# Block one's bands read q and k from the pooled branch's pieces; band matmuls in 64x64 and 128x64 tiles

## The chip, the cores and the metric

One core of a Trainium2 chip runs the whole program in one launch. The metric is the device time of one execution in microseconds, the median of three runs. The kernel before takes 1001.09 us (1000.05 to 1003.14).

## What is computed

Attention over 4 batches, 8 heads, 576 positions and 64 dimensions, followed by two expert layers (512 to 2048 to 512) on the 2304 tokens. The attention has two branches that are added. The pooled one averages q, k and v over groups of four positions and attends over 144; its result is repeated four times. The local one lets each position see only those less than four away:

```
q_d, k_d, v_d = mean over 4 positions of q, k, v
out_up    = repeat(softmax(q_d k_d' / 8) v_d, 4)
scores    = where(|i - j| < 4, q k' / 8, -1e9)
out_local = softmax(scores) v
x  = out_up + out_local                 # 2304 x 512
x  = relu(x @ w_in)^2 @ w_out           # layer 1
h  = x @ w2_in;  out = (h * cos(h)) @ w2_out   # layer 2
```

## The kernel before, in words

**Tiles.** Two heads lie on the 128 partitions (head pair hp of four, 64 dimensions each). The local branch goes by bands (`window(w)`): 64 query positions and the 70 keys around them (67 at a batch's edge), 9 bands a batch, 36 in all. A band loads one tile with q and k of all four pairs (`qkw`, L367) and one with v (`vw`, L372). In `qkw`, q of a pair stands as a 128x128 block with zeros off the diagonal, so that one 128x128 matmul scores both heads of a pair at once: rows 0 to 63 of the score bank are head one's positions, rows 64 to 127 head two's. L379 first writes the mask into the bank (identity times the band mask, bfloat16), L383 adds the scores, one float32 matmul for each pair. The softmax follows (`exps`, L273 to L290), the division on POOL (L393), the transposes of each pair (L403), the copy to SBUF (L406, `pt`), and L420 multiplies v with it, again 128x128 for each pair: of the output, the two diagonal 64x64 blocks are used. L436 adds the pooled result and writes x, L448 and L449 split x into a high and a low part.

**The pooled branch.** `pool(b)` loads q and k of a batch in eight pieces (128x576, one for each of q, k and pair, L200) and v in further pieces (L203), and VectorE sums groups of four (L260, L265, L267). `down(b, hp)` scores a pair (L303), transposes (L324), copies (L331, `dpt`), multiplies with v (L336) and copies the result out (L345, `xd`). A band's product with v waits until all four pairs of its batch are done.

**The layers.** `conv1(f)` loads a raw weight tile (1 MB, L461) and decodes it into a high and a low tile (L475 to L496). The main loop does, for each block of tokens and each of 16 weight tiles, 12 matmuls of `stage_a` (L568) and 12 of `stage_b1` (L620) or as many rows of `stage_b2` (L626). Block one of layer 1 is the first eight bands; the other 28 are computed beside the main loop's matmuls of earlier blocks, and are started at slots of that loop.

**Order.** Ahead of the main loop (`early[0]` is true) the program runs in rounds over a list of generators: `pool(0)`, four `down(0, hp)`, `window(0)` to `window(7)`, three `conv1`. Each goes on until it lacks a buffer or ends a stage. `need` and `done` count buffers (`caps`); in this phase the names in `SPREAD` may also take one of 13 spare tiles, those of weight tiles 3 to 15, which nobody has filled yet. Pooled pieces take only spare tiles, and give them back as soon as their sum is issued. Between the rounds a few matmuls on constants (`warm`, L697) are issued on TensorE. From this order the framework makes each engine's own program, by simulated times; at run time each engine keeps to its program and waits on semaphores. All DMAs are issued by SyncE (SP), in order.

Of the kernel before, what the change touches and what calls it, by code (L numbers as in the profile page):

```python
# [8 lines left out]
F32 = mybir.dt.float32  # L9
# [9 lines left out]
P = 128  # L19
B, H, S, D = 4, 8, 576, 64  # L20
FACTOR = 4
SD = S // FACTOR
HALO = FACTOR - 1
HPAIR = H // 2
WQ = 64
WK = WQ + 2 * HALO
# [27 lines left out]
TOP_MIN = 2.0 ** -15  # L54
TOP_MAX = (2.0 - 2.0 ** -3 - 2.0 ** -23) * 2.0 ** 16
LO_RING = (("loa", AHEAD), ("lob", AHEAD + LAG))
SPREAD = ("pl", "qkw", "vw", "dpr", "dpt")
RANK = {"down": 0, "window": 1, "pool": 2, "conv1": 3, "conv2": 3}


# [8 lines left out]
def kernel(  # L69
# [43 lines left out]

    caps = {
        "a": 3, "h": 1, "acc": 4, "qkw": 3, "vw": 3, "pr": 3, "pt": 2, "xt": 1, "qp": 1, "xd": 2, "vp": 1, "av": 3, "pl": 2, "raw": 2,
        "dpr": 2, "dpt": 1,
    }
    used = dict.fromkeys(caps, 0)
    now = [-1]
# [3 lines left out]

    def need(name, n=1):
        while early[0] and name in SPREAD:
            if name != "pl" and used[name] < caps[name]:
                used[name] += 1
                held.setdefault(name, []).append(None)
                return
            if spare:  # L130
                held.setdefault(name, []).append(spare.pop(0))
                return
            yield
        while used[name] + n > caps[name]:
            yield
        used[name] += n

    def done(name, n=1):
        f = taken[name].pop(0) if early[0] and name in SPREAD else None
        if f is None:  # L140
            used[name] -= n
        else:
            spare.append(f)
# [33 lines left out]


    pooled = {}
    xds = {}  # L180
    qk_used = {}
    vp_used = {}
# [5 lines left out]
    def pool(b):  # L188
        yield from need("qp")
        yield from need("vp")  # L190
        kp = cm.tile([P, HPAIR, SD], F32, tag="kp", name="kp", bufs=caps["qp"])
        vp = cm.tile([KTOK, 2, DM], F32, tag="vp", name="vp", bufs=caps["vp"])
        parts = [(i, hp) for hp in range(HPAIR) for i in range(2)]
        parts += [((0, 1), hp) for hp in range(HPAIR)] if early[0] else [((kt,), hp) for hp in range(HPAIR) for kt in range(2)]
        loaded = []
        for i, hp in parts:
            yield from need("pl")
            if isinstance(i, int):
                t = task_tile("pl", P, S)
                nc.sync.dma_start(out=t, in_=pool_qk[b, i, hp])  # L200
            else:
                t = task_tile("pl", KTOK, len(i) * FACTOR * P)
                nc.sync.dma_start(  # L203
                    out=t.rearrange("p (k c) -> p k c", k=len(i)),
                    in_=pool_v[b, hp, :, i[0]:i[-1] + 1],
                )
            loaded.append((i, hp, t))
            if len(loaded) < 2:
                continue
            if not early[0]:  # L210
                yield
            if b < PE_POOLED:
                if not early[0]:
                    yield
                bank, = yield from need_a()
                pe_pool(bank, loaded, kp, vp)
                done_a(bank)
                done("pl")
                done("pl")
                loaded = []  # L220
            while loaded:
                pool_sum(*loaded.pop(0), kp, vp)
                done("pl")
        pooled[b] = (qp, kp, vp)

    def pe_pool(bank, pieces, kp, vp):
# [25 lines left out]
    def pool_sum(*piece):  # L252
        with behind("gl", "xl"):
            pool_piece(*piece)
# [107 lines left out]
    def window(w):  # L362
        b, i, t0, k0, k1 = window_of(w)
        n, off = k1 - k0, HALO - (t0 - k0)
        yield from need("qkw")
        qk = task_tile("qkw", P, HPAIR * (2 * WQ + WK))
        nc.sync.dma_start(out=qk, in_=win_qk[w])  # L367
        qw = qk[:, :HPAIR * 2 * WQ].rearrange("p (h m) -> p h m", h=HPAIR)
        kw = qk[:, HPAIR * 2 * WQ:].rearrange("p (h s) -> p h s", h=HPAIR)
        yield from need("vw")  # L370
        vw = task_tile("vw", WK, DM)
        nc.sync.dma_start(out=vw, in_=win_v[w])  # L372
        yield
        if not early[0]:
            yield
        yield from need("pr")
        s, = yield from need_a()
        sv = s[:, :HPAIR * n].rearrange("p (h s) -> p h s", h=HPAIR)
        nc.tensor.matmul(  # L379
            sv, ident_b, band[:, off:off + n].unsqueeze(1).broadcast_to([P, HPAIR, n]), start=True, stop=False  # L380
        )
        for hp in range(HPAIR):
            last["pe"] = nc.tensor.matmul(  # L383
                sv[:, hp], qw[:, hp], kw[:, hp, :n], start=False, stop=hp == HPAIR - 1
            ).ins
        done("qkw")
        mx = cm.tile([P, 2, HPAIR], F32, tag="mx", name="mx", bufs=4)
        pr = cm.tile([P, HPAIR, WK], F32, tag="pr", name="pr", bufs=caps["pr"])
        prv = pr[:, :, :n]
        yield from exps(s, sv, mx, prv, SCALE)  # L390
        nc.vector.tensor_scalar_add(out=mx[:, 1], in0=mx[:, 1], scalar1=1e-9)
        nc.vector.reciprocal(out=mx[:, 1], in_=mx[:, 1])
        nc.gpsimd.tensor_tensor(  # L393
            out=prv, in0=prv, in1=mx[:, 1].unsqueeze(2).broadcast_to([P, HPAIR, n]), op=ALU.mult
        )
        yield
        if not early[0]:
            yield
        yield from need("pt")
        tp, = yield from need_a()  # L400
        tpv = tp.rearrange("p (h m) -> p h m", h=HPAIR)
        for hp in range(HPAIR):
            last["pe"] = nc.tensor.transpose(tpv[:n, hp], pr[:, hp, :n], ident).ins  # L403
        done("pr")
        pt = cm.tile([WK, HPAIR, P], F32, tag="pt", name="pt", bufs=caps["pt"])
        nc.scalar.copy(out=pt[:n], in_=tpv[:n])  # L406
        done_a(tp)
        yield
        while placed[0] < w:
            yield  # L410
        yield from need("av")
        j = max(n for n in range(NB) if W0[n] <= w)
        m = w - W0[j]
        while any((b, hp) not in downs for hp in range(HPAIR)):
            yield
        xh, xl = yield from x_tiles(j)
        av, = yield from need_a()
        avv = av.rearrange("p (h m) -> p h m", h=HPAIR)
        for hp in range(HPAIR):
            last["pe"] = nc.tensor.matmul(  # L420
                avv[:, hp], vw[:n, hp * P:(hp + 1) * P], pt[:n, hp], start=True, stop=True
            ).ins
        done("pt")
        done("vw")
        placed[0] += 1
        while any((b, hp) not in downs for hp in range(HPAIR)) or added[0] < w:
            yield
        if (j, m // 2) not in xts:
            yield from need("xt")
            xts[j, m // 2] = cm.tile([P, HPAIR, 2 * WQ], F32, tag="xt", name="xt", bufs=caps["xt"])  # L430
        xt = xts[j, m // 2]
        jd = WQ // FACTOR
        for a in range(2):
            rows = slice(a * D, (a + 1) * D)
            xa = xds[b][rows, :, i * jd:(i + 1) * jd].unsqueeze(3).broadcast_to([D, HPAIR, jd, FACTOR])
            nc.vector.tensor_tensor(  # L436
                out=xt[rows, :, (m % 2) * WQ:(m % 2 + 1) * WQ].rearrange("p h (j r) -> p h j r", r=FACTOR),
                in0=avv[rows, :, a * WQ:(a + 1) * WQ].rearrange("p h (j r) -> p h j r", r=FACTOR),
                in1=xa, op=ALU.add,
            )  # L440
        done_a(av)
        done("av")
        added[0] += 1
        if m % 2 or m == WINS1[j] - 1:
            m0 = m - m % 2
            cs = slice(m0 * WQ, (m + 1) * WQ)
            xv = xt[:, :, :(m % 2 + 1) * WQ]
            nc.scalar.activation(out=xh[:, :, cs], in_=xv, func=AF.Copy)  # L448
            last["xl"] = nc.vector.tensor_tensor(  # L449
                out=xl[:, :, cs], in0=xv, in1=xh[:, :, cs].bitcast(F32), op=ALU.subtract  # L450
            ).ins
            done("xt")
        ready.add(w)
# [388 lines left out]
def _layouts(inputs):  # L842
# [10 lines left out]
    pool_v = vt.reshape(B, 2, KTOK, FACTOR, HPAIR, P).transpose(0, 4, 2, 1, 5, 3).reshape(  # L853
        B, HPAIR, KTOK, 2, P * FACTOR
    )
    win_q = np.zeros((NW, P, HPAIR, 2, WQ), q.dtype)
    win_k = np.zeros((NW, P, HPAIR, WK), k.dtype)
    win_v = np.zeros((NW, WK, DM), v.dtype)
    for w in range(NW):
        b, i, t0, k0, k1 = window_of(w)  # L860
        for a in range(2):
            rows = slice(a * D, (a + 1) * D)
            win_q[w, rows, :, a] = qt[b, rows, :, t0:t0 + WQ]
        win_k[w, :, :, :k1 - k0] = kt[b, :, :, k0:k1]
        win_v[w, :k1 - k0] = vt[b, k0:k1]
    win_qk = np.concatenate([win_q.reshape(NW, P, -1), win_k.reshape(NW, P, -1)], axis=2)
# [40 lines left out]
```

## Time and profile before

| | |
|---|---|
| median of three runs | 1001.09 us |
| profiled execution | 1008.34 us, its span 1006.2 us |
| TensorE busy | 966.9 us, 96% |
| VectorE, ScalarE, GpSimd busy | 613.0, 462.7, 146.0 us |
| moved by DMA | 145.50 MB |

Columns of the views: PE is a matmul on TensorE, PEld a weight load beside it, DVE VectorE, ACT ScalarE, POOL GpSimd, SPq SyncE's issues. A float32 matmul leaves two records each of PE and PEld. Times are microseconds from the span's start; `x8` counts instructions merged in a row; what stands in brackets is the idle time of the engine ahead of it and what ended it. A busy time holds each instruction's whole length, from start to end, with overlaps counted once, while the chain counts each only from where the next one takes over. PEclk is the granted clock as a share of 2.4 GHz.

### The profile page before, as it was taken

What the parts mean: (1) busy time and instruction counts of PE and PEld (TensorE: products, weight loads), DVE (VectorE), ACT (ScalarE), POOL (GpSimd) and SP (SyncE); (2) the same over time, 40 slices, a digit from 0 to 9 for tenths busy, and PEclk for the clock granted to TensorE, in tenths of its full rate; (3) what the DMA queues carried; (4) which work ended last, traced back from release to release, by engine and by line L of the source; (5) the groups of instructions that cost most, each with busy time, mean ns of one, the idle gap of its engine ahead of it and who ended that gap; (6) DMA issues with size and microseconds to landing.
All of it is one profiled execution on the core that took longest, in us unless ns stands there. A gap on an engine that the chain in (4) does not pass through costs nothing.

```text
span 1006.2 us, 13030 instructions
## 1 busy us (share of the span) xinstructions
PE 966.9 (96%) x4820; PEld 825.4 (82%) x4820; DVE 613.0 (61%) x1050; ACT 462.7 (46%) x865; POOL 146.0 (15%) x112
## 2 busy tenths in 40 slices
PE   6797998989999999999999999999999999999998
PEld 4586776869999999999999898888888888888887
DVE  5358999966456854345237836556556655655565
ACT  3544565535544644454345644344334433433343
POOL 1312654502110311211002600000000000000000
PEclk8679998999999999999999999999999999999999
DMA  9834676677568956586356756002000100100010
GB/s 253 285 113 148 228 251 240 222 226 270 169 209 266 315 179 208 173 303 239 106 187 247 273 167 246 1 0 84 1 1 21 43 1 0 43 1 1 1 43 22
DMA packets 55936, 145.50 MB, mean 145 GB/s; under 512 B 6664, under 2 KB 9864, under 8 KB 51520
## 3 DMA queue, kind: packets, MB, share of 16 engines
q1 hardware_dynamic: 55872, 144.67, 42.5%
q8 instruction: 38, 0.62, 0.3%
q14 instruction: 26, 0.21, 0.1%
HBM read 116.33 MB, written 28.31 MB: 144 GB/s over the span
## 4 chain that ended last, share of the span: by engine, by line
PE 74%; DVE 7%; issue 2%; DMA 2%; ACT 0%; SPq 0%; DVEq 0%
PE ps_h L568 35%; PE acc L626 20%; PE acc L620 14%; DVE bits L482 2%; PE ps_a L420 2%; PE ps_a L383 2%; DVE bits L478 1%; DVE gl L586 1%; PE ps_a L403 1%; DMA pl<-in_pool_qk_dram 1%; DMA pl<-in_pool_v_dram 1%; PE ps_a L336 1%; DVE bits L477 1%; PE ps_a L303 1%; DVE bits L485 1%
## 5 line engine op out<-in xcount | busy, mean ns | idle before, releaser
L586 DVE TENSOR_TENSOR gl<-gt,gh 128x448 fp32r<-128x448 f32 (+1 forms) x80 | 59.9, 749 | 116.1 <-ACT gh L580 96.3
L568 PE MATMUL ps_h<-xh,w1hi 128*128 128x448 f32 (+1 forms) x320 | 122.7, 384 | 6.1 <-ACT gt L591 5.4
L620 PE MATMUL acc<-gl,w1hi 128*128 128x448 f32 (+1 forms) x320 | 121.4, 379 | 2.4 <-DVE gl L586 2.2
L568 PE MATMUL ps_h<-xl,w1hi 128*128 128x448 f32 (+1 forms) x320 | 120.9, 378 | 0.8 <-DVE xl L449 0.8
L568 PE MATMUL ps_h<-xl,w2hi 128*128 128x512 f32 (+1 forms) x320 | 117.3, 373 | 0.0
L568 PE MATMUL ps_h<-xh,w2hi 128*128 128x512 f32 (+1 forms) x320 | 117.2, 373 | 0.0
L608 ACT ACTIVATE r<-r,half_pi 128x512 f32<-128x512 f32 (+1 forms) x80 | 54.6, 683 | 135.6 <-DVE r L604 135.6
L626 PE MATMUL acc<-w2hi,gh 128*128 128x512 f32 x288 | 113.7, 395 | 0.0
L626 PE MATMUL acc<-w2lo,gh 128*128 128x512 f32 x288 | 113.4, 394 | 0.0
L626 PE MATMUL acc<-w2hi,gl 128*128 128x512 f32 x288 | 113.4, 395 | 0.0
L620 PE MATMUL acc<-gh,w1hi 128*128 128x448 f32 (+1 forms) x320 | 104.2, 381 | 3.7 <-ACT gh L580 3.7
L602 DVE TENSOR_SCALAR u<-u 128x512 f32<-128x512 f32 (+1 forms) x80 | 32.0, 400 | 118.5 <-ACT u L597 118.1
L620 PE MATMUL acc<-gh,lo 128*128 128x448 f32 x256 | 93.7, 366 | 0.0
L591 ACT ACTIVATE gt<-ps_h 128x448 f32<-128x448 f32 (+1 forms) x80 | 44.1, 552 | 85.0 <-PE ps_h L568 84.0
L568 PE MATMUL ps_h<-xh,w2lo 128*128 128x512 f32 (+1 forms) x320 | 80.4, 371 | 0.0
L597 ACT ACTIVATE u<-ps_h,quarter 128x512 f32<-128x512 f32 (+1 forms) x80 | 51.6, 645 | 47.8 <-PE ps_h L568 47.6
L568 PEld LDWEIGHTS ps_h<-xh,w1hi 128*128 128x128 f32 x320 | 61.0, 191 | 13.8 <-ACT gt L591 6.5
L580 ACT ACTIVATE gh<-r 128x512 fp32r<-128x512 f32 (+1 forms) x80 | 47.1, 589 | 51.7 <-DVE r L612 46.8
L568 PEld LDWEIGHTS ps_h<-xh,w2hi 128*128 128x128 f32 x320 | 60.1, 188 | 12.2
L568 PEld LDWEIGHTS ps_h<-xl,w2hi 128*128 128x128 f32 x320 | 60.1, 188 | 12.2
L620 PEld LDWEIGHTS acc<-gl,w1hi 128*128 128x128 f32 x320 | 60.9, 190 | 10.8 <-DVE gl L586 4.3
L620 PEld LDWEIGHTS acc<-gh,w1hi 128*128 128x128 f32 x320 | 60.2, 190 | 11.0 <-ACT gh L580 4.8
(111 smaller groups left out, 1831.5 us busy)
## 6 DMA issues: line engine op xcount, KB each, us to landing
raw<-in_w_dram SPq DMA_DIRECT2D x32, 1024.0 KB
lo<-lo_d SPq DMA_DIRECT2D x128, 256.0 KB
qkw<-in_win_qk_dram SPq DMA_DIRECT2D x36, 396.0 KB
pl<-in_pool_qk_dram SPq DMA_DIRECT2D x32, 288.0 KB
w_d<-shi SPq DMA_DIRECT2D x10, 512.0 KB
w_d<-bits SPq DMA_DIRECT2D x10, 512.0 KB
w2lo<-w_d SPq DMA_DIRECT2D x10, 512.0 KB
w2hi<-w_d SPq DMA_DIRECT2D x10, 512.0 KB
```

The lines of the kernel that those rows point to most:

```text
L383: last["pe"] = nc.tensor.matmul(sv[:, hp], qw[:, hp], kw[:, hp, :n], start=False, stop=hp == HPAIR - 1).ins
L420: last["pe"] = nc.tensor.matmul(avv[:, hp], vw[:n, hp * P:(hp + 1) * P], pt[:n, hp], start=True, stop=True).ins
L482: nc.vector.scalar_tensor_tensor(out=x, in0=low, scalar=29, in1=x, op0=ALU.logical_shift_right, op1=ALU.bitwise_or)
L568: nc.tensor.matmul(h[:, :n], a[:, c * P:(c + 1) * P], x[:, c, :n], start=i == 0, stop=i == len(order) - 1)
L580: nc.scalar.activation(out=gh, in_=gt, func=AF.Copy)
L586: last["gl"] = nc.vector.tensor_tensor(out=gl, in0=gt, in1=gh.bitcast(F32), op=ALU.subtract).ins
L591: last["relu"] = nc.scalar.activation(out=gt, in_=h, func=AF.Relu).ins
L597: nc.scalar.activation(out=u, in_=h, func=AF.Identity, bias=quarter, scale=float(1.0 / (2 * math.pi)))
L602: nc.vector.tensor_scalar(out=u, in0=u, scalar1=MAGIC, scalar2=MAGIC, op0=ALU.add, op1=ALU.subtract)
L608: nc.scalar.activation(out=r, in_=r, func=AF.Sin, bias=half_pi, scale=1.0)
L620: nc.tensor.matmul(acc[d][:, :n], a, x, start=f == 0 and i == 0, stop=f == NF - 1 and i == 2)
L626: nc.tensor.matmul(acc[t], x[:, ts], a[:, DM:2 * DM], start=f == 0 and i == 0, stop=f == NF - 1 and i == 2)
```

## The change

`pool(0)` keeps the eight q and k pieces of batch 0 (`qk0`, in spare tiles), and the eight bands of block one take their q and k from them as slices; they load no `qkw` and wait until all eight pieces are issued. A kept piece is given back when all eight bands have been scored. In all 36 bands q stands without zeros (`qkw` is 536 columns wide, not 792), and each matmul of a pair becomes two, one for each head: mask and scores on 64 rows and 64 output partitions (64x64 tiles on the diagonal), the product with v on all key rows and 64 output partitions (128x64 tiles).

```diff
--- before.py
+++ after.py
@@ -54,7 +54,7 @@
 TOP_MIN = 2.0 ** -15
 TOP_MAX = (2.0 - 2.0 ** -3 - 2.0 ** -23) * 2.0 ** 16
 LO_RING = (("loa", AHEAD), ("lob", AHEAD + LAG))
-SPREAD = ("pl", "qkw", "vw", "dpr", "dpt")
+SPREAD = ("qk0", "pl", "vw", "dpr", "dpt")
 RANK = {"down": 0, "window": 1, "pool": 2, "conv1": 3, "conv2": 3}
 
 
@@ -113,7 +113,7 @@
 
     caps = {
         "a": 3, "h": 1, "acc": 4, "qkw": 3, "vw": 3, "pr": 3, "pt": 2, "xt": 1, "qp": 1, "xd": 2, "vp": 1, "av": 3, "pl": 2, "raw": 2,
-        "dpr": 2, "dpt": 1,
+        "dpr": 2, "dpt": 1, "qk0": 0,
     }
     used = dict.fromkeys(caps, 0)
     now = [-1]
@@ -123,7 +123,7 @@
 
     def need(name, n=1):
         while early[0] and name in SPREAD:
-            if name != "pl" and used[name] < caps[name]:
+            if name not in ("qk0", "pl") and used[name] < caps[name]:
                 used[name] += 1
                 held.setdefault(name, []).append(None)
                 return
@@ -177,6 +177,8 @@
 
 
     pooled = {}
+    whole = {}
+    scored = set()
     xds = {}
     qk_used = {}
     vp_used = {}
@@ -194,8 +196,12 @@
         parts += [((0, 1), hp) for hp in range(HPAIR)] if early[0] else [((kt,), hp) for hp in range(HPAIR) for kt in range(2)]
         loaded = []
         for i, hp in parts:
-            yield from need("pl")
-            if isinstance(i, int):
+            keep = early[0] and isinstance(i, int)
+            yield from need("qk0" if keep else "pl")
+            if keep:
+                t = whole[i, hp] = task_tile("qk0", P, S)
+                nc.sync.dma_start(out=t, in_=pool_qk[b, i, hp])
+            elif isinstance(i, int):
                 t = task_tile("pl", P, S)
                 nc.sync.dma_start(out=t, in_=pool_qk[b, i, hp])
             else:
@@ -219,8 +225,10 @@
                 done("pl")
                 loaded = []
             while loaded:
-                pool_sum(*loaded.pop(0), kp, vp)
-                done("pl")
+                piece = loaded.pop(0)
+                pool_sum(*piece, kp, vp)
+                if not early[0] or piece[:2] not in whole:
+                    done("pl")
         pooled[b] = (qp, kp, vp)
 
     def pe_pool(bank, pieces, kp, vp):
@@ -362,11 +370,13 @@
     def window(w):
         b, i, t0, k0, k1 = window_of(w)
         n, off = k1 - k0, HALO - (t0 - k0)
-        yield from need("qkw")
-        qk = task_tile("qkw", P, HPAIR * (2 * WQ + WK))
-        nc.sync.dma_start(out=qk, in_=win_qk[w])
-        qw = qk[:, :HPAIR * 2 * WQ].rearrange("p (h m) -> p h m", h=HPAIR)
-        kw = qk[:, HPAIR * 2 * WQ:].rearrange("p (h s) -> p h s", h=HPAIR)
+        apart = early[0]
+        if not apart:
+            yield from need("qkw")
+            qk = cm.tile([P, HPAIR * (WQ + WK)], F32, tag="qkw", name="qkw", bufs=caps["qkw"])
+            nc.sync.dma_start(out=qk, in_=win_qk[w])
+            qw = qk[:, :HPAIR * WQ].rearrange("p (h m) -> p h m", h=HPAIR)
+            kw = qk[:, HPAIR * WQ:].rearrange("p (h s) -> p h s", h=HPAIR)
         yield from need("vw")
         vw = task_tile("vw", WK, DM)
         nc.sync.dma_start(out=vw, in_=win_v[w])
@@ -374,16 +384,30 @@
         if not early[0]:
             yield
         yield from need("pr")
+        while apart and len(whole) < 2 * HPAIR:
+            yield
         s, = yield from need_a()
         sv = s[:, :HPAIR * n].rearrange("p (h s) -> p h s", h=HPAIR)
-        nc.tensor.matmul(
-            sv, ident_b, band[:, off:off + n].unsqueeze(1).broadcast_to([P, HPAIR, n]), start=True, stop=False
-        )
+        halves_of = [slice(a * D, (a + 1) * D) for a in range(2)]
+        for rows in halves_of:
+            nc.tensor.matmul(
+                sv[rows], ident_b[rows, rows], band[rows, off:off + n].unsqueeze(1).broadcast_to([D, HPAIR, n]),
+                start=True, stop=False,
+            )
         for hp in range(HPAIR):
-            last["pe"] = nc.tensor.matmul(
-                sv[:, hp], qw[:, hp], kw[:, hp, :n], start=False, stop=hp == HPAIR - 1
-            ).ins
-        done("qkw")
+            for rows in halves_of:
+                if apart:
+                    qa, ka = whole[0, hp][rows, t0:t0 + WQ], whole[1, hp][rows, k0:k1]
+                else:
+                    qa, ka = qw[rows, hp], kw[rows, hp, :n]
+                last["pe"] = nc.tensor.matmul(sv[rows, hp], qa, ka, start=False, stop=hp == HPAIR - 1).ins
+        if apart:
+            scored.add(w)
+            if len(scored) == W0[1]:
+                for _ in range(2 * HPAIR):
+                    done("qk0")
+        else:
+            done("qkw")
         mx = cm.tile([P, 2, HPAIR], F32, tag="mx", name="mx", bufs=4)
         pr = cm.tile([P, HPAIR, WK], F32, tag="pr", name="pr", bufs=caps["pr"])
         prv = pr[:, :, :n]
@@ -415,11 +439,14 @@
             yield
         xh, xl = yield from x_tiles(j)
         av, = yield from need_a()
-        avv = av.rearrange("p (h m) -> p h m", h=HPAIR)
+        avv = av[:, :HPAIR * WQ].rearrange("p (h m) -> p h m", h=HPAIR)
         for hp in range(HPAIR):
-            last["pe"] = nc.tensor.matmul(
-                avv[:, hp], vw[:n, hp * P:(hp + 1) * P], pt[:n, hp], start=True, stop=True
-            ).ins
+            for a in range(2):
+                rows = slice(a * D, (a + 1) * D)
+                last["pe"] = nc.tensor.matmul(
+                    avv[rows, hp], vw[:n, hp * P + a * D:hp * P + (a + 1) * D], pt[:n, hp, a * WQ:(a + 1) * WQ],
+                    start=True, stop=True,
+                ).ins
         done("pt")
         done("vw")
         placed[0] += 1
@@ -435,7 +462,7 @@
             xa = xds[b][rows, :, i * jd:(i + 1) * jd].unsqueeze(3).broadcast_to([D, HPAIR, jd, FACTOR])
             nc.vector.tensor_tensor(
                 out=xt[rows, :, (m % 2) * WQ:(m % 2 + 1) * WQ].rearrange("p h (j r) -> p h j r", r=FACTOR),
-                in0=avv[rows, :, a * WQ:(a + 1) * WQ].rearrange("p h (j r) -> p h j r", r=FACTOR),
+                in0=avv[rows].rearrange("p h (j r) -> p h j r", r=FACTOR),
                 in1=xa, op=ALU.add,
             )
         done_a(av)
@@ -853,14 +880,12 @@
     pool_v = vt.reshape(B, 2, KTOK, FACTOR, HPAIR, P).transpose(0, 4, 2, 1, 5, 3).reshape(
         B, HPAIR, KTOK, 2, P * FACTOR
     )
-    win_q = np.zeros((NW, P, HPAIR, 2, WQ), q.dtype)
+    win_q = np.zeros((NW, P, HPAIR, WQ), q.dtype)
     win_k = np.zeros((NW, P, HPAIR, WK), k.dtype)
     win_v = np.zeros((NW, WK, DM), v.dtype)
     for w in range(NW):
         b, i, t0, k0, k1 = window_of(w)
-        for a in range(2):
-            rows = slice(a * D, (a + 1) * D)
-            win_q[w, rows, :, a] = qt[b, rows, :, t0:t0 + WQ]
+        win_q[w] = qt[b, :, :, t0:t0 + WQ]
         win_k[w, :, :, :k1 - k0] = kt[b, :, :, k0:k1]
         win_v[w, :k1 - k0] = vt[b, k0:k1]
     win_qk = np.concatenate([win_q.reshape(NW, P, -1), win_k.reshape(NW, P, -1)], axis=2)
```

## Rows read from the trace of the kernel before

**Rows 1.** Stretches: length; PE, PEld, DVE, ACT, POOL busy (count); PEclk, DMA share, GB/s.
```profile
0.00:82.00 82.00, 64.17 (x336) 50.25 (x336) 45.11 (x102) 36.00 (x133) 16.47 (x23) 0.77 0.65 202
82.00:224.00 142.00, 126.33 (x614) 101.22 (x613) 123.73 (x179) 75.86 (x130) 62.59 (x40) 0.95 0.68 228
224.00:520.00 296.00, 295.70 (x1663) 272.85 (x1664) 152.29 (x298) 142.30 (x268) 45.87 (x37) 0.99 0.64 218
```

**Rows 2.** Timeline of PE around 81 us: start, length, engine, line, operation.
```profile
81.52 0.50 PE L568 MATMUL ps_h<-xh,w1hi 128*128 128x512 f32 x1 [0.43 <-ACT xh L448]
```

**Rows 3.** The chain that ended last: shares, and pieces around 200 us.
```profile
PE 74%; DVE 7%; issue 2%; DMA 2%; ACT 0%; SPq 0%; DVEq 0%
...
194.93 4.26 DMA pl<-in_pool_qk_dram
```

**Rows 4.** Timeline of SP's issues at the front.
```profile
8.12 0.36 SPq L367 DMA_DIRECT2D qkw<-in_win_qk_dram  x1
...
25.03 0.35 SPq L367 DMA_DIRECT2D qkw<-in_win_qk_dram  x1
...
27.05 1.00 SPq L461 DMA_DIRECT2D raw<-in_w_dram  x2
```

**Rows 5.** Stretches of the front, columns as in rows 1.
```profile
10.00:27.00 17.00, 10.78 (x64) 9.32 (x62) 10.66 (x25) 6.71 (x37) 2.38 (x3) 0.79 0.99 247
27.00:38.00 11.00, 6.98 (x37) 4.75 (x36) 2.56 (x9) 3.89 (x19) 3.09 (x5) 0.81 1.02 333
...
39.30:62.00 22.70, 22.08 (x89) 18.42 (x90) 8.87 (x18) 10.65 (x33) 3.80 (x4) 0.50 0.40 142
...
65.00:82.00 17.00, 14.40 (x110) 11.96 (x107) 15.83 (x38) 9.03 (x28) 5.84 (x6) 1.00 0.36 124
```

**Rows 6.** Timeline of ACT around the first raw tile.
```profile
37.62 1.12 ACT L475 ACTIVATE bits<-raw 128x1024 f32<-128x1024 f32 x1 [6.44 <-DMA raw<-in_w_dram]
...
39.20 0.39 ACT L331 COPY dpt<-ps_acc 72x288 f32<-72x288 f32 x1
```

**Rows 7.** Timeline of PE at the front.
```profile
21.88 0.38 PE L379 MATMUL ps_acc<-const_b 128*128 128x268 bf16 x1 [6.22 <-ACT dpr L277]
...
39.27 1.15 PE L324 MATMUL ps_acc<-const_sb,dpr 96*72 96x96 f32 x6 [5.29 <-issue]
...
48.12 4.05 PE L336 MATMUL ps_acc<-dpt,vp 72*128 72x288 f32 x8
```

**Rows 8.** DMA issues from 10 to 27 us: count, KB each.
```profile
qkw<-in_win_qk_dram SPq DMA_DIRECT2D x7, 396.0 KB
```

**Rows 9.** Timeline of DVE, last sum of k, first and last of v.
```profile
11.02 0.75 DVE L265 TENSOR_REDUCE kp<-pl 128x144 f32<-128x576 f32 x1 [0.48 <-DMA pl<-in_pool_qk_dram]
...
12.67 1.22 DVE L267 TENSOR_REDUCE vp<-pl 72x256 f32<-72x1024 f32 x1 [0.90 <-DMA pl<-in_pool_v_dram]
...
17.71 1.22 DVE L267 TENSOR_REDUCE vp<-pl 72x256 f32<-72x1024 f32 x1 [0.58 <-DMA pl<-in_pool_v_dram]
```

**Rows 10.** Chain from 235 us: start, length, piece and count.
```profile
235.98 0.89 PE ps_a L420 x8
236.87 0.12 PE ps_a L379
236.99 0.84 PE ps_a L383 x8
...
238.29 0.25 PE ps_a L324 x3
...
241.28 0.74 PE ps_a L303 x6
```

**Rows 11.** Score matmuls from 200 to 520 us: ns, min/median/max.
```profile
L383 PE MATMUL ps_a<-qkw x152: 219/275/275, 218.8 to 501.5; 128*128 128x70 f32 x112, 128*128 128x67 f32 x40
```

**Rows 12.** Score matmuls by stretch: PE busy (count), PEld busy (count).
```profile
82.00:224.00 142.00, 6.98 (x56) 6.93 (x56) 0.95 0.68 228
224.00:520.00 296.00, 18.07 (x144) 17.68 (x144) 0.99 0.64 218
```

## The prediction

> **What bounds the kernel now.** Four views were read, in this order. The table of stretches first [rows 1]: from 224 to 520 us TensorE (PE) is busy 295.70 of 296 us; ahead of that it isn't, 64.17 of 82 us up to the first layer's start at 81.52 us [rows 2], and 126.33 of 142 us to 224 us. The chain that ended last, next [rows 3]: after 224.30 us it runs over PE instructions almost alone, so PE time there counts in full (PE holds 74% of the whole chain); in the stretch before, it runs over VectorE (DVE) work and over short waits for pooled pieces (4.26 us for one). Third the front, by SyncE's issues [rows 4] and the finer stretches [rows 5]: SP issues eight loads of a band's q/k, each with its v, from 8.12 to 25 us, and only then, at 27.05 us, the first two raw weight tiles, with the transfers 0.99 and 1.02 busy from 10 to 38 us. Last, who waited: ScalarE (ACT) stands 6.44 us for the first raw tile [rows 6], and PE 5.29 us until 39.27 us [rows 7], because the pooled branch's PSUM copies queue behind that wait on ACT. After this idle PE's granted clock is 0.50, the 1.2 GHz level, up to 62 us, while PE is busy 22.1 of 22.7 us [rows 5]; the first layer's first matmul comes 20 us later.
>
> So there are two questions: how much earlier the front ends, and what a band costs on PE where PE is the bound.
>
> **The front: transfers.** Eight q/k loads of 396 KB go [rows 8], 3.24 MB; at the 247 GB/s of 10 to 27 us [rows 5] that is 13.1 us of transfer. SP's next issues behind them, the v loads and the raw tiles, move up by as much; the raw tile that landed at 37.62 us [rows 6] is there by about 25 us. ACT was done with what precedes it at 31.18 us (37.62 - 6.44), so the whole wait goes and with it PE's idle: -5.3 us. Late next is ACT's own queue, so nothing more than the wait is taken. At the very start the four pooled v sums wait for their pieces, the first 0.90 us, the last 0.58 [rows 9], which share the transfers with q/k loads; the maxima behind them feed PE's wait at 21.88 us [rows 7]. Four waits of this size are 3 us; I take -1 (0 to -3).
>
> **The front: clock.** Without that idle PE need not fall to 1.2 GHz at 39 us. Its 22.1 busy us would be 11 at 2.4 GHz, if all of it were column time. But ACT and DVE feed these matmuls: at full clock, from 65 to 82 us, PE still idled 2.6 of 17 us [rows 5]; and the idle of 6.22 us ahead of 21.88 us, from which PE can come out slow as well, stays [rows 7]. Bounds 0 and -11 us; I take the middle, -5.5.
>
> **The front: what is added.** The kept q and k pieces take eight of the thirteen spare weight tiles until all eight bands are scored. Of the five that are left, two go to the probabilities of the third and fourth head pair (two have buffers of their own), three to v of bands 3 to 5. Nothing is left for a second transposed tile (one own buffer), so the pooled pairs' transposes go one at a time, some two rounds later, and v of bands 6 and 7, needed last, is issued behind them. Behind a held-up transpose stand, in PE's order, band scores, and later all products with v, which need the pooled result. A round is a pair's six transposes, two copies and four records of product: at the slow clock 1.15 + 2 x 0.39 + 4.05/2 = 3.95 us, at full clock some 2.4 [rows 6, 7]. From 0 (band work fills it) to two slow rounds, 7.9 us; I take one at full clock, +2.4, as PE has band scores to do meanwhile. Scores now wait for all eight pieces, but DVE had read those by 11.77 us [rows 9], and PE stands until 21.88 us in any case [rows 7]: nothing.
>
> Front: -5.3 - 1 - 5.5 + 2.4 = -9.4 us. It carries on: the stage behind starts its work by the main loop's steps, not by the hour.
>
> **The bands on PE.** A band's chain time now [rows 10]: eight records of score 0.84 us (0.105 each), mask 0.12, eight records with v 0.89 (0.111), 1.85 together. Each float32 matmul is two weight loads and two passes. What sets 0.105? 144 columns moved take 0.74/6 = 0.123 us, 96 take 0.25/3 = 0.083 [rows 10]: 0.86 ns a column. 70 columns would be 0.060, so the 128 weight columns set it, 0.82 ns each. After the change a band has 16 records of score with 64 weight columns (0.053) and 70 moved (0.060), two masks, and 16 with v at 64 and 64 (0.055). One after another: 0.96 + 0.24 + 0.88 = 2.08 us, +0.23. If the two halves run beside each other: 0.48 + 0.12 + 0.44 = 1.04, -0.81. And each band now goes four times from one tile size to another; no row of before shows one. Bounds of one: nothing, as between products, mask and scores now, where times add without a gap [rows 10], and 0.17 us, if the last matmul has to run out (0.275 from start to end [rows 11] less the 0.105 to the next). With all four that is 0.68, in all +0.91. I take one after another without a gap, the row nearest to it: +0.23.
>
> The Trainium skill, "TensorEngine Tiling (Array Packing)", section "Tiling Modes", says that changing the tiling mode drains TensorE. By that the four changes are paid in each band, the +0.91; by the row, which has no change of mode in it, nothing. The same section says that different tiles load weights and multiply in parallel; by that sentence a band would be the 1.04. No row can show either yet, so each is a rival below.
>
> Eighteen bands (144 of 288 score records, two passes by four pairs a band) lie after 224 us [rows 12]: 18 x 0.23 = +4 us; bounds -14.6 and +16.4. Seven lie between 82 and 224 us, under 15.7 us of PE's idle; there I cost the edit at nothing (without that cover, 7 x 0.23 = 1.6 us). The eleven of the front are in its bounds. The smaller later loads (268 for 396 KB) and the narrower source of the x sums are hidden: DVE's shapes stay, and after 224 us no transfer is in the chain.
>
> **Sum.** -9.4 + 4 = -5.4 us. The profiled execution took 1008.34 us (span 1006.2), the median is 1001.09, 0.7% less. 1002.9 by the profile is 996 us on the median's scale.
>
> **Rivals.**
> *The halves run side by side.* Then -9.4 - 14.6 = -24.0, 977 us. For it: weights, not columns, set the score's time, and the halves share neither rows nor output partitions. Against it: in the program both records of one half come before the other's.
> *Slower: a change of tile size is paid each time.* Place: the eighteen bands after 224 us, where nothing hides PE time. Price 0.91 us a band: +16.4 - 9.4 = +7.0, 1008 us. It decides from 9.4/18 = 0.52 us a band. For it: four changes for some 1 us of work each way; against it: between unlike shapes today nothing is lost.
> *The front gives little.* The five spare tiles hold back what the transfers gave, or the clock stays at 1.2 GHz, since it did so with PE busy throughout [rows 5]: front -3, bands +4, about 1002 us, no change. For it: DVE and ACT pace the bands from 65 to 82 us as it is. Against: the 6.44 us wait is on a load that leads the queue afterwards.
>
> **How the numbers follow.** Forecast 0.42, side by side 0.24, changes paid 0.18, little 0.16. The range, 977 to 1008 us, leaves out the tails of the two outer cases. Within 0.3% (3 us, about what can be told from no change) falls most of the last case and a little of the first: 0.18. Slower: the case of paid changes and a little of the last, 0.20. Faster 0.62.
>
> **What would show it.** In the profile after: the first main matmul near 72 us instead of 81.52; ACT without a wait for raw at the front; a granted clock over 0.5 from 40 to 60 us; the q/k issues of the first eight bands gone. In the chain after 224 us, a band's scores, masks and products with v should add to about 2.1 us; 1.0 is the first rival, 2.8 the second. The prediction is wrong if the first main matmul doesn't move, or if gaps beside the new tiles add up to more than the front gives.

## The result, and the profile after

| | before | after |
|---|---|---|
| median, same session | 1000.57 us (998.62 to 1003.14) | 985.86 us (983.05 to 986.93) |
| profiled execution, span | 1008.34, 1006.2 us | 986.93, 985.0 us |
| first main matmul | 81.52 us | 66.75 us |
| block one of layer 1, from there to the issue of the transfer of its result y | 148.2 us | 137.7 us |
| TensorE busy | 966.9 us | 940.7 us |
| moved by DMA | 145.50 MB | 138.67 MB |

The ratio is 0.983 [0.980, 0.987], 14.7 us less: inside the forecast's range and on its side, but nearly three times the 5 us of the forecast. The profiled execution of before lies 7.3 us above its median, at a mean granted clock of 0.973 where the median of 70 executions beside the experiments is 0.982, and that of after 1.1 above, at 0.984 where ten have 0.983; so the two spans differ by 21 us, and sizes below are taken from medians where there are any.

The stretches after, columns as in [rows 1]:

```profile
0.00:82.00 82.00, 61.30 (x575) 42.36 (x576) 55.86 (x121) 43.82 (x149) 21.42 (x26) 0.90 0.61 191
82.00:224.00 142.00, 126.63 (x757) 101.01 (x756) 121.07 (x182) 76.26 (x131) 62.45 (x39) 0.95 0.71 238
224.00:520.00 296.00, 293.55 (x2008) 263.87 (x2007) 153.94 (x291) 146.31 (x274) 44.03 (x36) 1.00 0.61 210
```

PE is about as busy as before in each, so the gain isn't idle time that went; the same stretches hold more of the work. The finer ones of the front, against [rows 5]:

```profile
10.00:27.00 17.00, 8.74 (x84) 6.89 (x83) 11.64 (x24) 5.80 (x27) 1.42 (x2) 0.78 0.97 281
27.00:38.00 11.00, 8.39 (x88) 5.79 (x86) 7.24 (x16) 8.92 (x36) 7.35 (x8) 0.88 0.77 249
39.30:62.00 22.70, 19.13 (x236) 13.34 (x235) 15.48 (x43) 14.20 (x61) 3.22 (x5) 0.97 0.10 26
65.00:82.00 17.00, 14.61 (x103) 11.39 (x104) 13.27 (x22) 9.80 (x18) 6.39 (x5) 0.90 0.74 253
```

From 39.3 to 62 us the granted clock is 0.97 where it was 0.50, and PE issues 236 records in place of 89 in 19.13 busy us for 22.08 (though a band's scores, masks and products now leave twice as many). SP's issues, against [rows 4]:

```profile
8.51 2.12 SPq L382 DMA_DIRECT2D vw<-in_win_v_dram  x3
12.12 2.04 SPq L488 DMA_DIRECT2D raw<-in_w_dram  x2
...
29.50 0.35 SPq L488 DMA_DIRECT2D raw<-in_w_dram  x1
```

The first two raw tiles are issued at 12.12 us, not 27.05. On ACT and PE, against [rows 6, 7] and [rows 2]:

```profile
23.00 1.13 ACT L502 ACTIVATE bits<-raw 128x1024 f32<-128x1024 f32 x1
...
35.52 1.12 ACT L502 ACTIVATE bits<-raw 128x1024 f32<-128x1024 f32 x1 [2.04 <-DMA raw<-in_w_dram]
```

```profile
23.12 0.43 PE L393 MATMUL ps_acc<-const_b 64*64 64x268 bf16 x2 [7.46 <-ACT dpr L285]
...
66.75 0.49 PE L595 MATMUL ps_h<-xh,w1hi 128*128 128x512 f32 x1 [2.54 <-ACT xh L475]
```

ACT takes its first raw tile without a wait (2.04 us are left, on the third), and PE's 5.29 us idle ahead of 39.27 is gone. PE's first idle, though, is longer: 7.46 us, ending at 23.12, where it was 6.22 and 21.88. The pooled sums, against [rows 9], are late too:

```profile
12.12 0.75 DVE L273 TENSOR_REDUCE kp<-qk 128x144 f32<-128x576 f32 x1 [0.95 <-DMA qk<-in_pool_qk_dram]
13.82 1.22 DVE L275 TENSOR_REDUCE vp<-pl 72x256 f32<-72x1024 f32 x1 [0.94 <-DMA pl<-in_pool_v_dram]
...
18.95 1.22 DVE L275 TENSOR_REDUCE vp<-pl 72x256 f32<-72x1024 f32 x1 [0.48 <-DMA pl<-in_pool_v_dram]
```

The four v sums wait as before (0.94 to 0.48 us), and the last starts 1.24 us later than at [rows 9]; 1.10 us of that is there at the last sum of k already.

The bands. Two pieces of the chain after 224 us, against [rows 10]: start, length, piece and count.

```profile
227.05 0.61 PE ps_a L446 x16
227.67 0.23 PE ps_a L393 x2
227.90 0.47 PE ps_a L403 x16
...
276.87 0.62 PE ps_a L446 x16
277.48 0.24 PE ps_a L393 x2
277.72 0.49 PE ps_a L403 x16
```

A band is 0.61 + 0.23 + 0.47 = 1.31 us to 1.35, where it was 1.85. It has twice the records, so each is short in the chain: 0.47/16 = 0.029 us a score record, against 0.105. Yet a score matmul itself takes, by its records from 224 to 520 us (ns, min/median/max):

```profile
L403 PE MATMUL ps_a<-qkw x288: 216/219/223, 227.7 to 480.0; 64*64 64x70 f32 x112, 64*64 64x67 f32 x32
```

So records of 219 ns follow each other every 29 ns. By their starts, the two records of a pair (head one's and head two's) begin 3 to 4 ns apart, and the next two 56 to 61 ns later, which is about the 0.060 us that the forecast gave 70 columns: the halves do run side by side.

The chain gives the length from where one piece takes over from the one ahead, so what a change of tile size costs lies partly in its neighbours. PE's timeline around one band has it:

```profile
245.02 0.57 PE L595 MATMUL ps_h<-xh,lo 128*128 128x448 f32 x2
245.52 0.31 PE L393 MATMUL ps_a<-const_b 64*64 64x280 bf16 x2
245.66 0.28 PE L403 MATMUL ps_a<-qkw 64*64 64x70 f32 x4
```

The first four score records start at 245.66 and have ended by 245.94. From start to start, medians in ns over the bands from 215 to 580 us whose products, mask and scores stand in a row between main matmuls (14 before, 10 after):

| | before | after |
|---|---|---|
| last main matmul to first product | 202 | 290 |
| first to last product | 779 | 463 |
| last product to mask | 112 | 152 |
| mask to first score | 123 | 143 |
| first to last score | 729 | 435 |
| last score to next main matmul | 79 | 148 |
| that to the second main matmul | 289 | 310 |
| the whole | 2313 | 1942 |

Products follow each other by 66 ns a pair on the mean (463/7; the second pair starts 107 ns after the first, the others 58 to 59), scores by 62; so at the change from products to mask 152 - 66 = 86 ns go, ahead of the products 88, and behind the scores 69 + 21. It is some 0.09 us a change (the 107 ns of the second pair not counted), and there are three in such a band, since mask and scores share a size; the prediction had four. The sum is 0.37 us less a band, -6.7 us for eighteen.

### The profile page after: what moved, and what is told of

Same layout as the page of the kernel before. It is cut to its first block, busy times and chain, and to the rows that moved or that the text cites. A ratio compares the mean times of both kernels' runs of the same rounds, so it can differ in the third digit from the quotient of the medians.

```text
span 985.0 us, 14253 instructions
## 1 busy us (share of the span) xinstructions
PE 940.7 (95%) x5436; PEld 788.1 (80%) x5436; DVE 612.5 (62%) x1050; ACT 462.4 (47%) x865; POOL 149.2 (15%) x112
## 2 busy tenths in 40 slices
DMA packets 54789, 138.67 MB, mean 141 GB/s; under 512 B 6536, under 2 KB 9736, under 8 KB 50368
## 4 chain that ended last, share of the span: by engine, by line
PE 74%; DVE 12%; DMA 6%; issue 4%; ACT 2%; POOL 1%; SPq 0%; POOLq 0%; DVEq 0%; ACTq 0%
PE ps_h L595 34%; PE acc L653 20%; PE acc L647 13%; DMA pl<-in_pool_v_dram 3%; DVE bits L509 2%; DVE bits L512 2%; DVE gl L613 2%; DVE bits L505 1%; DMA raw<-in_w_dram 1%; PE ps_a L446 1%; DVE bits L504 1%; PE ps_a L427 1%; PE ps_a L344 1%; PE ps_a L403 1%; DVE vp L275 1%
## 5 line engine op out<-in xcount | busy, mean ns | idle before, releaser
L613 DVE TENSOR_TENSOR gl<-gt,gh 128x448 fp32r<-128x448 f32 (+1 forms) x80 | 57.8, 722 | 94.4 <-ACT gh L607 78.2
L595 PEld LDWEIGHTS ps_h<-xl,w1hi 128*128 128x128 f32 x320 | 61.7, 193 | 7.0 <-DVE xl L476 0.9
```

Of the source, the lines that this page charges most:

```text
L595: nc.tensor.matmul(h[:, :n], a[:, c * P:(c + 1) * P], x[:, c, :n], start=i == 0, stop=i == len(order) - 1)
L613: last["gl"] = nc.vector.tensor_tensor(out=gl, in0=gt, in1=gh.bitcast(F32), op=ALU.subtract).ins
```

## The experiments

All were timed in five rounds beside the kernel before; each line gives the median, that of before on the same chip, and the ratio.

**The two parts, one by one.** *e1_front* keeps the pieces for block one's bands and has the old 128x128 tiles elsewhere: the scores of the 28 later bands (with the zeros loaded), all masks of those, and all products with v. One line of its edit:

```diff
-        for rows in halves_of:
+        for rows in halves_of if apart else [slice(0, P)]:
```

> Kept pieces alone: the first eight bands slice q and k from the pooled pieces (scores in 64x64 tiles, since they have no zeros), the other 28 bands and all products with v stay as before. Theory (the front gives some 15 us at the first main matmul and most of it stays; the tiles give some 0.37 us for each of 18 bands, of which part is given back): first main matmul near 67 to 69 us, time 988 to 991 us against 1000.6. Rival (the tiles carry the gain): 995 us or more. Rival (the tiles give nothing in the end): 986, as the whole change.

992.41 us against 1004.27, 0.990 [0.986, 0.994]: -10.3 us (11.9 by the medians alone), as the theory had it for the time, but the first main matmul comes at 75.72 us, 5.8 earlier, and not at 67 to 69. Its clock from 39.3 to 62 us:

```profile
39.30:62.00 22.70, 20.95 (x196) 16.96 (x194) 14.24 (x40) 13.68 (x59) 2.61 (x4) 0.97 0.09 27
```

Another 7.6 us come in block one of layer 1 (140.6 us against 148.2). Both are read against the profiled execution of before, and the two spans differ by 16.7 us, not 10.3.

*e2_tiles* has the tiles in all bands and keeps no piece; every band loads 268 KB.

```diff
-SPREAD = ("qk0", "pl", "vw", "dpr", "dpt")
+SPREAD = ("pl", "qkw", "vw", "dpr", "dpt")
...
-            keep = early[0] and isinstance(i, int)
+            keep = False
...
-        apart = early[0]
+        apart = False
```

> Tiles alone: all bands in 64x64 and 128x64 tiles and q without zeros, but the first eight bands load their own q and k (268 instead of 396 KB each), and no pooled piece is kept. Theory: a band's chain time after 224 us falls from 1.85 to about 1.33 us, and with changes of tile size counted by 0.37 us; 18 bands give 6.6 us at most; the raw tiles come 4 us earlier as 1 MB less stands ahead of them, so part of the wait for them goes too: 991 to 995 us. Rival (the front is all): 998 to 1001 us. Rival (bands carry all): 986 us.

997.38 against 1004.27, 0.994 [0.991, 0.997]: -6.4 us (6.9 by the medians alone). With e1 that is about -17; *a2_after*, the changed kernel once more, measured -17.1 on its chip (985.67 against 1002.78, 0.983 [0.979, 0.987]). Within intervals of some 4 and 3 us the parts add; the scores of the first eight bands are in small tiles in both.

> The changed kernel unaltered, as the base for the three runs beside it and for the spread of its profile. All theories: ratio to before 0.980 to 0.987. Theory (what the front wins is partly taken or given by the first block of layer 1, whose length depends on how raw tiles and pooled pieces arrive, not on the program alone): first main matmul within 1 us of 66.75 again, but the end of that block (204.5 us in the first profile) may move by several us.

The first main matmul of a2 came at 68.13 us, 1.4 later than in the first profile.

In e2 the first main matmul comes 10.7 us earlier (70.82), but block one of layer 1 then takes 154.4 us, six longer than before: that lead is given back. What the lead is made of isn't shown: eleven bands of the front have the tiles, the eight q/k loads are smaller by 1 MB, and the clock is high where the profiled execution of before had it low:

```profile
39.30:62.00 22.70, 18.18 (x250) 12.96 (x250) 12.46 (x35) 14.51 (x57) 6.97 (x8) 0.95 0.48 155
```

*e10_late_tiles* is the kernel before with the tiles in the 28 later bands only (q stays with its zeros, and loads are unchanged).

```diff
+        halves_of = [slice(0, P)] if w < W0[1] else [slice(a * D, (a + 1) * D) for a in range(2)]
...
```

> The kernel before with the tiles in the 28 later bands alone: loads, zeros and the first eight bands as before, later bands' mask and scores in 64x64 and products with v in 128x64 tiles. It splits what the tiles alone gave (6.4 us, with the first main matmul at 70.8 instead of 81.5). Theory (the front's bands count as much, PE being busy at half the clock there): front unchanged, first main matmul 81 to 82 us; 18 bands x 0.37 = 6.6 us at most after 224 us, in part given back: ratio 0.993 to 0.998. Rival (the later bands are all of it): 0.992 to 0.994 and the front's gain is lost again in the block behind it.

994.23 against 1000.87, 0.994 [0.992, 0.997]: -5.9 us with the front as it was:

```profile
39.30:62.00 22.70, 22.11 (x106) 16.92 (x105) 9.64 (x20) 10.46 (x33) 3.79 (x4) 0.50 0.43 149
...
82.24 0.49 PE L573 MATMUL ps_h<-xh,w1hi 128*128 128x512 f32 x1 [1.14 <-ACT xh L453]
```

Within the interval, that is what the records' starts give (-6.7), and all that the tiles are worth in e2 too.

**The front: bytes or order?** *e5_raw_early* is the kernel before with the first raw loads issued ahead of most of the band loads; no byte less.

```diff
+    first = [tasks[:8] + tasks[13:15] + tasks[8:13] + tasks[15:]]
     while tasks:
-        for t in list(tasks):
+        for t in first.pop() if first else list(tasks):
```

> The kernel before with one change of order: the first two raw weight tiles are issued behind the loads of the third band, ahead of those of bands 3 to 7; no byte is removed, no tile changed. Theory (the front's loss was the wait for the raw tile in ACT's queue and the slow clock after it): the wait of 6.4 us and PE's idle of 5.3 us go, the granted clock stays over 0.9 from 40 to 60 us, the first main matmul moves from 81.5 to 70 us or less, time 989 to 993 us. Rival (it is the transfers removed that count): first main matmul within 3 us of 81.5, time 998 to 1001.

1008.18 against 1004.27, 1.005 [1.002, 1.007], slower: the first theory fell, and the rival had no loss either. The first main matmul comes at 79.28 us. ACT's wait for the raw tile goes, and PE gets one for the bands' own loads in its place, then the low clock as before. PE's waits, in all, times and longest:

```profile
PE ps_a L383 <- DMA qkw<-in_win_qk_dram: 4.6, 1, 4.6
```

```profile
39.30:62.00 22.70, 21.09 (x87) 18.05 (x88) 5.44 (x17) 5.73 (x24) 1.31 (x2) 0.52 0.40 144
```

*e3_bytes* is the changed kernel with twelve loads that nobody reads put back beside the bands' v loads: 12 x 268 KB = 3.2 MB, the bytes taken away.

```diff
+        if apart:
+            for _ in range(2 - w % 2):
+                dead = cm.tile([P, HPAIR * (WQ + WK)], F32, tag="qkw", name="dead", bufs=caps["qkw"])
+                nc.sync.dma_start(out=dead, in_=win_qk[w])
```

> The changed kernel with the transfers that it saved put back: twelve loads of 268 KB that nobody reads, issued with the first eight bands' loads of v (3.2 MB, as much as the eight loads of 396 KB); tiles and kept pieces unchanged. Theory (what the kept pieces win is transfer time at the front, where the queue is full until some 35 us): the 5.8 to 10 us of the kept pieces are lost again, ratio to before 0.991 to 0.994, that of the tiles alone. Rival (the bytes don't count, the order of issue does): 0.982 to 0.985, as the changed kernel.

1001.58 against 1000.87, 1.000 [0.998, 1.002]: more is lost than either theory had, 17 us against the changed kernel. The transfers are full again up to 38 us (0.93 from 27 us on, for 0.77), and the clock is down:

```profile
10.00:27.00 17.00, 11.36 (x106) 8.46 (x103) 11.90 (x29) 6.58 (x31) 2.83 (x4) 0.90 0.99 271
27.00:38.00 11.00, 7.63 (x72) 5.20 (x72) 5.93 (x13) 7.82 (x32) 6.29 (x6) 1.00 0.93 285
39.30:62.00 22.70, 15.73 (x191) 10.78 (x191) 6.39 (x22) 11.07 (x47) 2.61 (x4) 0.85 0.48 149
65.00:82.00 17.00, 11.70 (x105) 7.97 (x103) 16.69 (x32) 7.43 (x20) 5.69 (x5) 0.63 0.40 133
```

The first main matmul comes at 78.98 us, though the first raw tile is issued at 15.88. That speaks for the bytes and against the order of issue, but isn't proof: the twelve loads also take the `qkw` buffers and move the plan, so not all 17 us need be theirs, and e1 had given only 10.3 for the kept pieces.

**The tiles: side by side, and at what price?** *e6_grouped* is the changed kernel with the records of each half in a row: head one's of all pairs, then head two's, in scores and products.

```diff
-        for hp in range(HPAIR):
-            for rows in halves_of:
+        for rows in halves_of:
+            for hp in range(HPAIR):
```

> The changed kernel with the halves grouped: the four pairs of head one, then the four of head two, for scores and for products with v; the matmuls are the same, only their order differs. Theory (the two halves run side by side because neighbours in the queue are on different tiles): without such neighbours the 16 score records take 0.96 us instead of 0.44 to 0.58, those with v 0.88 instead of 0.47 to 0.61, so +0.9 us a band, 16 us for the 18 bands after 224 us: near 1002. Rival (64 weight columns and 64 output partitions are faster by themselves, whatever the order): no change, 985 to 987. Between: the queue looks far enough ahead to pair some of them.

1001.26 against 1002.78, 0.998 [0.995, 1.000]: 15.6 us over the changed kernel on the same chip, so nearly the whole gain is lost by the order of eight instructions. A band in its chain, and on PE's timeline:

```profile
228.92 0.90 PE ps_a L446 x16
230.05 0.76 PE ps_a L403 x15
```

```profile
228.85 0.97 PE L446 MATMUL ps_a<-pt,vw 67*64 67x64 f32 x16
229.89 0.92 PE L403 MATMUL ps_a<-qkw 64*64 64x67 f32 x16
```

0.90 looks like the 0.88 that the forecast had for the products one after another, but it holds the change to the mask as well. By the starts, first to last product is 745 ns (463 in the changed kernel) and first to last score 735 (435): in each run of sixteen records, three start within 10 ns of another, where in the changed kernel it is eight. So PE still runs some of the two halves together, the case "between" of the expectation, and a band loses 0.58 us and not 0.9; 18 bands give 10.4 of the 15.6 us, and that the time came out near 1002 was luck in part. Where the rest goes isn't shown. To run all of them together, neighbours in the program had to lie on different tiles.

*e7_pv128* has the product with v as it was, 128x128, and the rest of the change.

```diff
...
-                    avv[rows, hp], vw[:n, hp * P + a * D:hp * P + (a + 1) * D], pt[:n, hp, a * WQ:(a + 1) * WQ],
...
+                avv[:, hp], vw[:n, hp * P:(hp + 1) * P], pt[:n, hp], start=True, stop=True
...
```

> The changed kernel with the product with v in 128x128 again, mask and scores still in 64x64 tiles. Theory (pairs side by side save, each change of tile size costs some 0.09 us): v goes from 0.031 us a record of 16 to 0.111 of 8, the change ahead of it goes, the one behind it stays: +0.27 us a band, 5 us for the 18 bands after 224 us, 990 to 992. Rival (the drains eat what the v tiles win): 984 to 987.

994.03 against 1002.78, 0.991 [0.988, 0.994]: 8.4 us over the changed kernel, more than the 5 expected, although one change of tile size goes; by the starts a band takes 2221 ns, 0.28 us more, which is 5.0 us for 18. The products are back at 0.89 in its chain:

```profile
268.78 0.89 PE ps_a L444 x8
269.67 0.24 PE ps_a L393 x2
269.91 0.49 PE ps_a L403 x16
```

**Repairs of what the prediction held against the change.** *e4_spare* gives a second buffer to the pooled branch's transposed tile, *e9_pr5* five buffers instead of three to the probabilities; both are otherwise the changed kernel. The edit of e4:

```diff
-        "dpr": 2, "dpt": 1, "qk0": 0,
+        "dpr": 2, "dpt": 2, "qk0": 0,
```

> The changed kernel with a second own buffer for the pooled branch's transposed tile, which it lost to the kept pieces. If holding the spare tiles costs what the prediction put on it (2.4 us, a round at full clock), 983 to 984 us against 986; if other work fills the rounds, 985 to 987 us, with the first main matmul within 1 us of 66.75.

> The changed kernel with five instead of three buffers for the bands' probabilities, so that bands 3 to 7 may be scored before the pooled branch is done and the kept pieces go back earlier. If the holding of the pieces costs anything at the front: first main matmul 1 to 3 us before 66.8 to 68.1, ratio 0.979 to 0.982. Rival (DVE and ACT pace the bands there): no change, 0.981 to 0.985. A second rival, from the runs with one buffer or some matmuls more: the planner's other order alone costs 5 to 10 us, 0.988 to 0.993.

e4: 994.33 against 1004.27, 0.993 [0.990, 0.996]. e9: 995.08 against 1000.87, 0.995 [0.994, 0.997]. By the ratios they are about 10 and 12 us slower than the changed kernel, which neither expectation had as its theory. In e9 the front has a wait that the changed kernel hasn't; its PE waits:

```profile
PE ps_acc L427 <- POOL pr L417: 9.4, 1, 9.4
```

In the changed kernel that wait is 4.0 us in two, and the first main matmul of e9 comes at 77.67 us. In e4 it comes at 68.89, only 2.1 later, and the loss lies in block one (154.8 us). More buffers make the planner order the program otherwise; that this order costs the time is argued, and no run isolates it. Whether the spare tiles cost the forecast's 2.4 us isn't told by these; that adding these buffers does not help is.

*e8_warm* puts 28 matmuls on constants behind the first round, against the low clock that PE still has from 22 to 28 us.

```diff
+    rounds = 0
...
-            warm(WARM)
+            warm(WARM if rounds else 28)
+        rounds += 1
```

> The changed kernel with 28 instead of 4 matmuls on constants behind the first round, in the stretch from 15.7 to 23.1 us in which PE waits for ACT. Theory (that idle takes the granted clock to 0.50 from 22 to 28 us, and the front pays for it): clock 1.0 from 22 to 28 us, first main matmul 1 to 3 us before 66.75, time 983 to 985. Rival (ACT and DVE set the pace there, not PE): first main matmul within 1 us, time unchanged.

991.23 against 1002.78, 0.988 [0.984, 0.991]: 5.6 us over the changed kernel, with the first main matmul at 72.85 us, 6.1 later: neither expectation held. The clock from 22 to 28 us rises, and falls later, where it had been full (first fence the changed kernel, second e8):

```profile
22.00:28.00 6.00, 4.08 (x60) 3.76 (x61) 4.36 (x15) 6.00 (x26) 2.42 (x2) 0.50 0.90 317
34.00:39.00 5.00, 3.25 (x52) 2.66 (x50) 1.48 (x5) 3.21 (x7) 1.87 (x3) 1.00 0.43 161
```

```profile
22.00:28.00 6.00, 3.54 (x55) 3.18 (x55) 4.52 (x13) 5.94 (x26) 1.52 (x2) 0.68 0.92 329
34.00:39.00 5.00, 4.16 (x23) 2.50 (x24) 1.51 (x8) 4.76 (x25) 1.94 (x3) 0.54 0.31 111
```

## Why the prediction was right in sign and short in size

**The step that failed: "I take one after another without a gap, the row nearest to it: +0.23"** a band. It is -0.37 by the starts, and -5.9 us measured for the late bands (e10) where the sum had +4. Nothing in the trace of before could decide it, as the text said; what misled was the argument against the rival, that in the program both records of one half come before the other's. They do, but PE starts the other half's within 4 ns all the same. Both rivals' mechanisms were true at once: side by side (e6, e7), and a price for each change of tile size, some 0.09 us and not the bound of 0.17. Scores, masks and products side by side were to save 0.81; three changes take back 0.26, and products follow every 66 ns on the mean where the forecast had 55, 0.09 more. Masks (143 ns for 123) and scores (62 for 60) are some 0.04 of what is left to -0.37; the other 0.05 aren't accounted for. Of the two sentences of the Trainium skill ("TensorEngine Tiling (Array Packing)", section "Tiling Modes"), the trace after agrees with both: 3 to 4 ns between the starts of two scores (6 to 7 of two products), and 86 to 90 ns more at each change.

**Front, transfers: -5.3.** Right in its way. The raw issues moved from 27.05 to 12.12 us (14.9 us, for the 13.1 worked out), ACT's 6.44 us wait went, and PE's 5.29 us with it. e5 shows that the place in the queue alone wins nothing; that it is the bytes fits e3, whose loads move the plan as well.

**Front, pooled v waits: -1.** Wrong in sign: +1.2, of which 1.10 stood at the last sum of k. The v pieces wait as long as before, without the q/k loads behind them; the transfers are as full with the raw tiles in their place (0.97 for 0.99), and which loads set the wait no run isolates.

**Front, clock: -5.5.** In the profile the clock stayed at 0.97 from 39.3 to 62 us, but at the medians the size isn't borne out. The rows that the term was read from are of an execution of 1008.34 us at a mean clock of 0.973. In the 70 executions of before beside the experiments, a mean lower by 0.01 goes with some 8.4 us more; beside a2 the median of the mean clock is 0.981 for before and 0.983 for the changed kernel, which by that is under 2 us. Whether the usual execution of before has the low stretch from 39.3 us at all isn't shown.

**Front, spare tiles: +2.4.** Not shown: two kernels that give tiles back were slower.

**Sum of the front: -9.4.** e1 measures -10.3. That the two are near is luck in part: of the four terms the first is borne out, the second had the wrong sign, the third hardly shows in the medians, and the fourth is not shown. In e1's profile 5.8 us stand at the first main matmul, and 7.6 come in block one of layer 1. The sentence "it carries on: the stage behind starts its work by the main loop's steps" was too simple: that block took from 134.8 to 154.8 us among the kernels run here. (By PE's last matmul of the block, which ends at 227.97 us before and at 198.18 after, it is 146.5 and 131.4 us: 4.5 us more stand there, and block two gives them back, with 109.7 us for 103.2.) Part of it is work that changes place: after the change, blocks three to five of layer 1 hold the products with v of fourteen bands instead of twelve, the scores of thirteen instead of eleven and those of one pooled pair more, and take 273.1 us instead of 269.8.

**Bands up to 224 us: nothing.** The eleven of the front were "in its bounds" without a price; in e2, with tiles and smaller loads, the first main matmul came 10.7 us earlier, and block one gave it back. For the time, nothing was about right: e10, with the first eight bands as before, gains as much as e2.

So -9.4 + 4 should have been -10.3 - 6.4 or so. What stays open: why block one of layer 1 is 154 us in the profiles of e2 and e4 (executions 3.8 and 6.5 us above their medians) and 138 after the change. The order of the plan differs, and no run isolates what in it counts.

## What to carry to other kernels

Where a matmul leaves half of the array's columns, or half of its rows and columns, without use, two small tiles side by side took 0.6 of the time here (62 ns for 105, 66 for 111), if neighbours in the program lay on different tiles; count the changes of tile size beside it, at some 0.09 us each here, and put what shares a size in a row. Where a stage's transfers are full (0.99 here), taking bytes away paid and moving an issue forward only moved the wait. Before a cost is read from one execution's clock, put its mean clock beside those of the others. A gain at the start of a planned loop is a gain at its end only as far as the next block doesn't give it back: take the milestones of the blocks, and not just the first.

## What had not been expected of the hardware and the program

The order of the two loops over pairs and halves was worth 15.6 us of 986 with the same instructions (e6), and yet PE ran some of the two halves together in the worse order too. A record's length says nothing of its cost on PE when tiles run together: 219 ns long, one every 29. And one more buffer for one tile went with about 10 us more (e4), two more for another with 12 (e9), probably by the plan that came of it.
